# One table of the order of all steps, made anew with other step times for three kinds of steps: attention and two mixtures on one core

## The chip, the cores and the metric

The kernel runs on one core of one Trainium2 chip. What counts is the device time of one execution in microseconds (us), from the first to the last instruction with what the runtime puts around it; the figure of a kernel is the median over its runs.

## What is computed

The inputs are q, k and v for 4 batches of 8 heads, 576 positions and 64 columns, a vector s for each head, and the weights of two feed-forward layers over all 2304 tokens. The reference, cut to what matters (the causal mask, reshaping and small constants are left out):

```python
bias   = cum[..., None, :] - cum[..., :, None]          # cum: running sum of max(s, 0)
scores = q @ k.T / 8 + minimum(bias, 0)                  # causal
attn   = softmax(scores) @ v                             # then x = heads side by side, 2304 x 512

h = x @ w_in                                             # 512 -> 2048
x = (h - tanh(h)) @ w_out                                # 2048 -> 512

h = x @ w2_in                                            # 512 -> 1024
e = exp(h - max(h)); solu = h * e / sum(e)
out = layernorm(solu) * g_ln @ w2_out                    # 1024 -> 512
```

## The kernel before

**Number form.** A float32 operand is split into a high part (a cast to the matmul's own 32-bit form) and a low part (what the cast leaves), and each product is three matmuls: high by high, high by low, low by high. So almost every value that TensorE makes is read out of PSUM by ScalarE (ACT) or VectorE (DVE), cast ("hi"), and subtracted ("lo") before TensorE (PE) may use it again. `copy` (L293 and its neighbours) and `diff` (L317 on VectorE, L318 on GpSimd) are the helpers for that, so that those lines collect work of all stages.

**Attention.** Twenty jobs A0 to A19 (pairs of heads; the first eight jobs are two halves of one pair) of units with scores (L719), the bias and maximum (L736), the exponential (L747), row work on GpSimd (POOL, L751), transposes (L785) and the product with v in `weigh` (L825, after which `xs` at L835 and a store to DRAM give the next layer's input). During it the weights of the next layer are loaded in float32 ("cd") and split (`convert_w`, L403 to L421; the first instruction of a split is an ACT absolute value at L421, `ct<-cd`).

**First layer** (`expert1`). Nine blocks of 256 tokens. A step *h* of one chunk of 128 hidden columns is 12 matmuls of 256 columns (L872, into `t`); then come tanh on ACT (L877), the gate h - tanh h on VectorE (L881), the cast to `gh` on ACT (L293), the low part on VectorE or GpSimd (L317, L318), and two chunks later a step *x* of 12 matmuls (L895) into an accumulator. Chunks 0 to 7 run in two visits (Xa) into `acc`, some of them while attention still runs; their sums are kept in DRAM. Chunks 8 to 15 run last (Xb) into `big`, and `join` (L957, `xp`) adds the kept sums. The weights of chunks 8 to 15 (tiles `wb`) have no room until attention's buffers are given up: `att_close` does that after the last attention step, and their loads are issued behind it.

**Second layer.** For each block, `products` P0 to P8 forms the hidden values with seven products instead of eight (p1, p6, p5, p2, p3, p7, p4 in program order), each 6 matmuls of 512 columns (L1013). p1 and p2 add into one half of the PSUM tile `big`, p5 and p3 into the other; p6, p7 and p4 use a tile `b`. Between them stand small steps: copies of p1 and p5 to `hc` on ACT (k1, k5), the sum u2 (L1029), k15 (`hc<-hc`, L317), and u4 at L1044, which adds u2 into the half of `big` that p5 wrote and that p3 will add to. The weights of this layer are split by the same engines shortly before P0. `expert2`, E0 to E17 (128 tokens each), does the softmax form, the layernorm statistics and the reciprocal root: an integer first guess (L1100 to L1102) and three rounds of three tiny instructions on 128x1 tiles, `newton` (L1107 to L1109), on GpSimd or on VectorE. Its result is used by `fin` alone (ACT, L1134), after the four product steps *o* (L1129) of that tile; before those the tile is transposed (step *T*, L1115), cast and split (`cu`, `cd`, L1122).

**What sets the order.** Nothing is decided on the chip. `schedule` creates 3302 steps with their dependencies, and `Plan.order` reads the string `ORDER`: each base-36 word is three times the number of a step plus the number of the way it is done (which engine); `+n` is n filler matmuls on a tile `junk` (L562), which compute nothing that is used. The steps are emitted in that order, and each engine works off its instructions in the order in which they were emitted. The costs that stand in the calls of `add` and `any` are inputs of a planner that is not part of this file: here they are read by nothing that emits instructions.

Of the kernel before, what the change touches and what calls it, by code (L numbers as in the profile page):

```python
# [43 lines left out]
TB = 256  # L44
# [17 lines left out]
35o vi su wf vg vl wd vo wi sx v6 wl vr 11x 12o 13r 123 wo 12u wx 126 12r 129 399 vu 121 12y 130 13u 12c x0 vx 133 wr
140 159 x3 144 136 wu 13x 139 16f 146 13i 15c t6 149 15i 11r 12f 15f 15m 13c 14c 16i 13l 14o 13f 1rx 15o 16o x6 14f
15r 12i 16r 13o 14r 183 15u 34o x9 166 14i xf 14u ul xj 15x 16u 1eo 34r xl 34u 14l 1s0 34x xc 160 xo uo 350 169 163
18c 14x ur 353 xr xu 16c 18f uu 196 356 150 1f0 16l xx y3 153 16x 3df 35r 170 35u 39c 17c y0 y6 156 18i 3di 199 3dx
173 19f 18o 3dl 36l 19l 18m 18r 39f 3do 18u 39i 17l y9 17f 18x 1ex 3e0 1f3 176 3e3 3ds 19c 190 19o 17i yc 19r 39l 179
1a3 1ac 1f9 1l9 39o 17o 1bu 3e6 193 19u 1fc 1af 39r 1ll 1ff 1al 3ea 379 17r 1ai 1bx 3er 1fi 1ar 1ap 39u 3h0 1c0 1au
1f7 1ax 19j yf 1c3 1b9 36o 19x yi 3ef 1b0 1c9 yl 36r 1cc 17u 1c7 1cf 17x 1li 1a0 1ci 1a6 1b3 1a9 36u 1bc 1fl 1cr 1b6
1fr 1bf 36x 1bi 1fo 180 1fu 1lo 1gx 1fx 1ls 370 1if 1lu 1g0 37x 373 1lx 1h0 1cl 376 37c 1cu 1h3 1io 3ei 1cx 1ii 1g6
1g4 37f 1co 1g9 1m0 1d0 37i 1iu 1m3 1h6 1ha 3el 1is 37l 1m6 1yi 3eu 1d9 1m9 3eo 37o 1bl 1hc 1bo 37r 1d3 3f9 3ex 37u  # L70
1d6 3f0 3fo 1gc 3f3 1hf 1dc 1gf 1hi 3fc 3f6 1il 1br 1hu 3ff 3g6 1ix 3fi 1go 1j0 3b9 3fl 3fr 1jc 1df 3fu 1ru 3g3 1di
1hl 3fx 1dl 3g0 3g9 1dx 3gc 1yl 3gl 3gf 1do 3gi 380 1j3 1e0 383 1e6 1dr 1e3 386 1gi 3h3 1du 389 1gl 1e9 38c 1mc 3h6
38l 1ni 3h9 38f 1mf 1ec 3hc 1ml 3hf 1mi 1nr 1mr 1nv 1mu 1nx 38i 1nl 3bc 1mp 1gr 1s3 1mx 3bf 1ef 1hx 1n9 1ei 1ho 1gu
# [1239 lines left out]
```

## Time and profile before

| what | value |
| --- | --- |
| median of 3 runs | 791.61 us (791.07 to 792.75) |
| the profiled execution | 792.16 us |
| its span, first to last instruction | 790.4 us |
| PE busy | 771.3 us (98%) |
| DVE, ACT, POOL busy | 541.4, 412.6, 156.0 us |
| mean granted clock of TensorE | 0.999 of full speed |

The profile shows one execution. An engine counts as busy while an instruction of its runs; a matmul's end is modelled, so that a busy PE can still run its matmuls further apart or closer together. 1.76 us of the profiled execution lie outside the span. The waits are inferred from semaphores: a row "PE x <- DVE y" is time in which PE stood still until that instruction of VectorE was done.

### The profile page before, as it was taken

How to read it: one execution, taken by the hardware profiler on the slowest of the kernel's cores; microseconds unless marked ns; L12 is line 12 of the kernel's file. 1: busy time of each engine (PE TensorE's matmuls, PEld its weight loads, DVE VectorE, ACT ScalarE, POOL GpSimd, SP SyncE). 2: the span in 40 equal slices, each digit the busy share in tenths (PEclk: the TensorE clock that was granted, in tenths of full speed). 3: DMA queues.
4: the chain of work that ended last, by engine and by line, in shares of the span. 5: the costliest groups of instructions: out<-in, count | busy, mean ns of one | idle time of the engine just before them, and what ended most of it. 6: DMA issues, size and time to landing. Idle time of an engine off the chain costs nothing.

```text
span 790.4 us, 16621 instructions
## 1 busy us (share of the span) xinstructions
PE 771.3 (98%) x6235; PEld 681.0 (86%) x6235; DVE 541.4 (68%) x1521; ACT 412.6 (52%) x1028; POOL 156.0 (20%) x321
## 2 busy tenths in 40 slices
PE   8899999999999999999999999999999999999998
PEld 5565788888898899999999898888899899989876
DVE  6887988854554366985699998765465664564773
ACT  6779988766666445554355664333142333333332
POOL 4334433322331100000000001122041202021112
PEclk9999999999999999999999999999999999999999
DMA  6999979867445379875445431012012101201001
GB/s 189 300 284 252 329 219 290 271 184 215 123 121 165 105 226 292 278 244 181 160 131 183 136 111 48 15 54 92 16 43 65 41 15 66 95 1 41 15 27 41
DMA packets 90033, 111.90 MB, mean 142 GB/s; under 512 B 11792, under 2 KB 74256, under 8 KB 89952
## 3 DMA queue, kind: packets, MB, share of 16 engines
q1 hardware_dynamic: 89952, 110.83, 45.7%
q8 instruction: 49, 0.80, 0.4%
q14 instruction: 32, 0.26, 0.1%
HBM read 87.11 MB, written 23.70 MB: 140 GB/s over the span
## 4 chain that ended last, share of the span: by engine, by line
PE 80%; DVE 10%; ACT 4%; DMA 2%; issue 2%; SPq 1%; POOL 0%; ACTq 0%; DVEq 0%; POOLq 0%
PE t L872 20%; PE t L1129 12%; PE acc L895 11%; PE big L895 10%; PE big L1013 6%; PE t L825 5%; PE t L785 4%; PE b L1013 4%; PE t L719 4%; PE t L1115 2%; ACT U L747 1%; DVE ct L414 1%; DVE U L736 1%; DVE ct L409 1%; ACT pt L293 1%
## 5 line engine op out<-in xcount | busy, mean ns | idle before, releaser
L872 PE MATMUL t<-xb,wih 128*128 128x256 f32 x1152 | 203.4, 279 | 0.1
L872 PEld LDWEIGHTS t<-xb,wih 128*128 128x128 f32 x1152 | 175.6, 188 | 2.2 <-DVE m L736 0.3
L872 PE MATMUL t<-xb,wil 128*128 128x256 f32 x576 | 160.0, 278 | 0.0
L751 POOL TENSOR_SCALAR U<-U,r 128x256 f32<-128x256 f32 (+8 forms) x144 | 85.8, 608 | 174.5 <-DVE r L663 72.9
L872 PEld LDWEIGHTS t<-xb,wil 128*128 128x128 f32 x576 | 108.7, 189 | 0.0
L895 PE MATMUL acc<-gh,woh 128*128 128x256 f32 x576 | 104.7, 283 | 1.2 <-DVE gh L317 1.1
L895 PE MATMUL big<-gh,woh 128*128 128x256 f32 x576 | 101.2, 278 | 0.6 <-DVE xp L957 0.6
L881 DVE TENSOR_TENSOR g<-t,th 128x256 f32<-128x256 f32 x144 | 59.8, 418 | 52.4 <-ACT th L877 51.2
L293 ACT CAST gh<-g 128x256 fp32r<-128x256 f32 x144 | 58.0, 406 | 67.9 <-DVE g L881 30.1
L877 ACT ACTIVATE th<-t 128x256 f32<-128x256 f32 x144 | 55.0, 383 | 71.1 <-PE t L872 66.5
L895 PEld LDWEIGHTS acc<-gh,woh 128*128 128x128 f32 x576 | 87.7, 188 | 3.0 <-DVE gh L317 1.8
L747 ACT ACTIVATE U<-U,m 128x256 f32<-128x256 f32 (+8 forms) x144 | 80.3, 559 | 18.4 <-DVE m L736 17.8
L895 PEld LDWEIGHTS big<-gh,woh 128*128 128x128 f32 x576 | 87.9, 188 | 1.8 <-ACT th L877 0.7
L317 DVE TENSOR_TENSOR gh<-g,gh 128x256 fp32r<-128x256 f32 x130 | 56.4, 436 | 36.2 <-ACT gh L293 35.0
L895 PE MATMUL acc<-gh,wol 128*128 128x256 f32 x288 | 80.4, 279 | 0.2 <-DVE wol L317 0.2
L895 PE MATMUL big<-gh,wol 128*128 128x256 f32 x288 | 79.9, 278 | 0.0
L293 ACT COPY pt<-t 128x512 f32<-128x512 f32 (+4 forms) x160 | 61.2, 427 | 14.1 <-PE t L785 13.1
L736 DVE CUSTOM_DVE_ANT_0 U<-bc,t 128x256 f32<-128x256 f32 (+8 forms) x144 | 60.2, 441 | 5.7 <-PE t L727 3.0
L719 PE MATMUL t<-kn,q 64*64 64x288 f32 (+8 forms) x640 | 59.3, 422 | 1.8 <-ACT pt L293 0.9
L895 PEld LDWEIGHTS acc<-gh,wol 128*128 128x128 f32 x288 | 54.5, 189 | 0.4 <-DVE wol L317 0.4
L895 PEld LDWEIGHTS big<-gh,wol 128*128 128x128 f32 x288 | 54.2, 188 | 0.0
L1107 POOL TENSOR_SCALAR u<-y,va 128x1 f32<-128x1 f32 x45 | 20.9, 465 | 165.1 <-DVE y L1102 137.9
(115 smaller groups left out, 1432.5 us busy)
## 6 DMA issues: line engine op xcount, KB each, us to landing
xb<-xd SPq DMA_DIRECT2D x17, 1024.0 KB, 7.2
cd<-in_moe_w_in_dram SPq DMA_DIRECT2D x24, 512.0 KB, 5.5
cd<-in_moe_w_out_dram SPq DMA_DIRECT2D x24, 512.0 KB, 4.8
bc<-cum_d SPq DMA_DIRECT2D x32, 288.0 KB, 6.4
pd<-xp SPq DMA_DIRECT2D x18, 512.0 KB, 3.0
xp<-pd SPq DMA_DIRECT2D x18, 512.0 KB, 4.1
xd<-xs SPq DMA_DIRECT2D x16, 320.0 KB, 5.1
kn<-in_k_dram SPq DMA_DIRECT2D x16, 288.0 KB, 5.2
```

Of the source, the lines that this page charges most:

```text
L293: nc.scalar.copy(o, i)
L317: return self.any([("dve", t_dve(n, pair=True), lambda: nc.vector.tensor_tensor(*views(), op), "diff-dve"), ("pool", t_pool(n) + split, la ...
L719: nc.tensor.matmul(X[a][c, :z - a], lhsT=V["q"][r, o:o + 64], rhs=V["k"][r, a:z], start=True, stop=True, skip_group_check=True)
L736: nc.vector.tensor_tensor_reduce(out=X["u"][:, a:z], in0=V["bc"][:, n, a:z], in1=X[b][:, a - b:z - b], scale=-0.125, scalar=X["m"] if "m" ...
L747: nc.scalar.activation(out=X["u"][:, :nk], in_=X["u"][:, :nk], func=AF.Exp, scale=-1.0, bias=X["m"], accum_out=Y["s"][:, n:n + 1])
L751: eng.tensor_scalar(X["u"][:, :nk], X["u"][:, :nk], Y["r"][:, n:n + 1], 1.0, ALU.mult, ALU.mult)
L872: nc.tensor.matmul(ps, lhsT=w[l][:, k, f * 128:f * 128 + 128], rhs=xb[:, r, k, :], start=k == 0 and x == 0, stop=k == 3 and x == 2)
L877: nc.scalar.activation(out=X["th", f], in_=X["h", f], func=AF.Tanh)
L881: nc.vector.tensor_tensor(X["g", f], X["h", f], X["th", f], ALU.subtract)
L895: nc.tensor.matmul(X["acc"][:, m, :], lhsT=w[l][:, f, m * 128:m * 128 + 128], rhs=X["gh", f][:, r, :], start=f == c0 and m % 2 == 0 and x ...
L1013: nc.tensor.matmul(o, lhsT=self.x2[j][:, l, x, k], rhs=r[:, b, k, :], start=start and k == 0 and n == 0, stop=k == 1 and n == 2, skip_grou ...
L1129: nc.tensor.matmul(X["po"], lhsT=X["lt", k // 4][:, l, k % 4, :], rhs=r[:, k, :], start=k == 0 and a == 0, stop=k == 7 and a == 2)
```

## The change

The string `ORDER` is another one. Beside it the costs of three kinds of steps are changed: the h and x steps of `expert1` from 1405 to 1370 ns, the products and the output steps of the second layer from 1360 to 1366 ns, and `newton` on GpSimd from 1900 to 3200 ns. As nothing that emits instructions reads the costs, the program differs by the table alone. Of the table the diff is cut to its first line; lines behind the table stand one further down.

```diff
-0 f x 3 i 10 l u 49 7x p 4i r +22 13 4l 1u 16 2i 86 1a 1c 1x 39 bu 2l 20 2p 6 1f 23 2r 1i 3c 89 1l 2u 4d 26 2x bx 4f
...
+0 f 3 u i l x 49 4i 7x p r +20 13 10 1u 2i 16 86 1a 1c 1x 39 bu 2l 4d 6 2p 1f 20 3c 4l 2r 23 1i 4f 1l 89 3f 2u 26 2x
...
-                s = add("pe", t_pe(1405.0, 12 * TB), lambda f=f: h_part(f), ld + [w["ready"][2 * f]] + list(deps), acq=("ps",),
+                s = add("pe", t_pe(1370.0, 12 * TB), lambda f=f: h_part(f), ld + [w["ready"][2 * f]] + list(deps), acq=("ps",),
...
-                s = add("pe", t_pe(1405.0, 12 * TB), lambda f=f2: x2_part(f), [glo[f2], w["ready"][2 * f2 + 1]],
+                s = add("pe", t_pe(1370.0, 12 * TB), lambda f=f2: x2_part(f), [glo[f2], w["ready"][2 * f2 + 1]],
...
-            s = add("pe", t_pe(1360.0, 3072), go, deps + list(self.w2_all), acq=acq, rel=rel)
+            s = add("pe", t_pe(1366.0, 3072), go, deps + list(self.w2_all), acq=acq, rel=rel)
...
-        y = self.any([("pool", 1900, lambda: newton(nc.gpsimd), "rstd-pool"), ("dve", 2170, lambda: newton(nc.vector), "rstd-dve")],
+        y = self.any([("pool", 3200, lambda: newton(nc.gpsimd), "rstd-pool"), ("dve", 2170, lambda: newton(nc.vector), "rstd-dve")],
...
-            s = add("pe", t_pe(1360.0, 3072), lambda k=k: prod(k), [los[k // 4], self.w2_ready[8 + k], self.w2_ready[9 + k]],
+            s = add("pe", t_pe(1366.0, 3072), lambda k=k: prod(k), [los[k // 4], self.w2_ready[8 + k], self.w2_ready[9 + k]],
```

What the new table moves, counted over all steps: TensorE has the same 739 steps and 53 fillers instead of 49 (at the start 20 instead of 22). `newton` is on VectorE in all 18 tiles, where it was on GpSimd in 15 and on VectorE in 3. Of the `diff` steps 35 instead of 26 are on GpSimd. Two copies go from GpSimd to ACT.

**The last block of the second layer, PE.** `big` is the tile that p1, p2, p5 and p3 write, four rows each; `t<-idn,ct` are transposes of two tiles' halves. Before, from the end of p5 on:

```order
L1013 MATMUL big<-w2ih,x_10333 128x512 x2
L1013 MATMUL big<-w2il,x_10333 128x512
L1115 MATMUL t<-idn,ct 128x128 x8
L1013 MATMUL big<-w2ih,x_10333 128x512 x2
L1013 MATMUL big<-w2il,x_10333 128x512
L1013 MATMUL big<-w2ih,x_10333 128x512 x2
L1013 MATMUL big<-w2il,x_10333 128x512
L1013 MATMUL big<-w2ih,x_10333 128x512 x2
```

The last row is the start of p3, and the four rows ahead of it are p2. In the changed kernel, from p2 on:

```order
L1014 MATMUL big<-w2ih,x_10351 128x512 x2
L1014 MATMUL big<-w2il,x_10351 128x512
L1014 MATMUL big<-w2ih,x_10351 128x512 x2
L1014 MATMUL big<-w2il,x_10351 128x512
L1116 MATMUL t<-idn,ct 128x128 x8
L1014 MATMUL big<-w2ih,x_10351 128x512 x2
```

The transposes that stood ahead of p2 now stand between p2 and p3. In P0 to P8 there stood between p2 and p3: h, nothing, nothing, x, nothing, four h, h, two o, nothing. Now: h; two T, h and o; two T, three x and three h; thirteen steps; nothing; six h; two x; nothing; two T. In P4, P7 and P8 of the changed kernel (and in P4 before) u4 is emitted ahead of p2.

**The end of attention, ACT.** `xp<-acc` is the copy of a block's sums, and `ct<-cd` the first instruction that needs a weight loaded after `att_close`. Before:

```order
L293 COPY xp<-acc 128x1024
L877 ACTIVATE th<-t 128x256
L293 CAST gh<-g 128x256
L877 ACTIVATE th<-t 128x256
L421 ACTIVATE ct<-cd 128x512
L877 ACTIVATE th<-t 128x256
L293 CAST gh<-g 128x256 x2
```

In the changed kernel:

```order
L294 COPY xp<-acc 128x1024
L878 ACTIVATE th<-t 128x256
L294 CAST gh<-g 128x256
L878 ACTIVATE th<-t 128x256
L294 CAST gh<-g 128x256
L878 ACTIVATE th<-t 128x256
L422 ACTIVATE ct<-cd 128x512
L878 ACTIVATE th<-t 128x256 x2
```

One cast and one tanh of the first layer now stand ahead of the first instruction that needs the new weight.

**The last tile, VectorE.** Ahead of the low parts `cd` and `cu` of tile E17, before:

```order
L1092 BN_AGGR mv<-bn 128x2
L1100 TENSOR_SCALAR va<-mv 128x1
L1101 TENSOR_SCALAR y<-va 128x1
L1102 TENSOR_SCALAR y<-y 128x1
L1095 TENSOR_SCALAR ct<-ct,mv 128x1024
L1122 TENSOR_TENSOR cd<-t,cd 128x512
```

In the changed kernel:

```order
L1093 BN_AGGR mv<-bn 128x2
L1096 TENSOR_SCALAR ct<-ct,mv 128x1024
L1101 TENSOR_SCALAR va<-mv 128x1
L1102 TENSOR_SCALAR y<-va 128x1
L1103 TENSOR_SCALAR y<-y 128x1
L1108 TENSOR_SCALAR u<-y,va 128x1
L1109 TENSOR_SCALAR u<-u 128x1
L1110 TENSOR_TENSOR y<-y,u 128x1
```

After its last row two more rounds of the same three instructions follow, and then `cd` and `cu`. These nine stood on GpSimd.

## Rows read from the trace of the kernel before

**Rows 1.** The page: busy time of the engines; the chain's shares.

```profile
PE 771.3 (98%) x6235; PEld 681.0 (86%) x6235; DVE 541.4 (68%) x1521; ACT 412.6 (52%) x1028; POOL 156.0 (20%) x321
PE 80%; DVE 10%; ACT 4%; DMA 2%; issue 2%; SPq 1%; POOL 0%; ACTq 0%; DVEq 0%; POOLq 0%
```

**Rows 2.** Busy time by stretch; columns: length, five engines, granted clock, DMA share, GB/s.

```profile
0.00:40.00 40.00, 34.59 (x322) 22.58 (x323) 28.69 (x134) 28.22 (x91) 15.74 (x38) 1.00 0.85 247
40.00:80.00 40.00, 37.63 (x371) 25.39 (x371) 32.79 (x126) 33.29 (x94) 16.36 (x25) 1.00 1.00 266
...
280.00:300.00 20.00, 18.79 (x159) 18.13 (x158) 15.45 (x34) 9.61 (x23) 0.74 (x1) 1.00 0.75 238
300.00:340.00 40.00, 40.00 (x348) 40.00 (x347) 31.22 (x66) 20.42 (x45) 0.75 (x1) 1.00 0.86 281
...
400.00:440.00 40.00, 40.00 (x335) 39.23 (x334) 38.35 (x86) 22.98 (x51) 1.64 (x2) 1.00 0.40 123
...
520.00:560.00 40.00, 39.40 (x246) 35.02 (x247) 23.67 (x48) 11.91 (x23) 8.85 (x21) 1.00 0.18 60
```

**Rows 3.** PE's waits over the span: total us, times, longest us.

```profile
PE big L1013 <- DVE big L1044: 5.0, 6, 1.4
...
PE acc L895 <- DVE gh L317: 1.1, 2, 0.6
```

**Rows 4.** Timeline in P8, VectorE and PE: start, duration, instruction, idle before.

```profile
760.16 0.39 PE L1013 MATMUL big<-w2il,x 128*128 128x512 f32 x1
760.59 0.70 DVE L1044 TENSOR_TENSOR big<-big,u 128x512 f32<-128x512 f32 x1 [1.02 <-PE big L1013]
761.34 0.73 PE L1013 MATMUL big<-w2ih,x 128*128 128x512 f32 x2 [0.79 <-DVE big L1044]
```

**Rows 5.** Timeline in P0, the steps between p2 and p3.

```profile
442.67 0.58 ACT L293 COPY hc<-big 128x512 f32<-128x512 f32 x1
443.41 0.68 DVE L317 TENSOR_TENSOR hc<-hc 128x512 f32<-128x512 f32 x1
444.75 0.73 PE L1013 MATMUL big<-w2ih,x 128*128 128x512 f32 x2 [1.37 <-DVE big L1044]
```

**Rows 6.** Timeline of ACT at the end of attention.

```profile
279.94 0.39 ACT L877 ACTIVATE th<-t 128x256 f32<-128x256 f32 x1
283.87 0.67 ACT L421 ACTIVATE ct<-cd 128x512 f32<-128x512 f32 x1 [3.55 <-DMA cd<-in_moe_w_in_dram]
```

**Rows 7.** Timeline of PE in the same place.

```profile
286.05 0.39 PE L895 MATMUL acc<-gh,woh 128*128 128x256 f32 x1 [0.51 <-DVE gh L317]
...
288.26 0.39 PE L895 MATMUL acc<-gh,woh 128*128 128x256 f32 x1 [0.55 <-DVE gh L317]
```

**Rows 8.** The chain that ended last, in order of time: start, duration, what.

```profile
277.93 5.70 DMA cd<-in_moe_w_in_dram
...
297.01 5.44 PE acc L895 x48
...
331.47 5.65 PE acc L895 x48
...
402.14 7.19 PE t L872 x60
```

**Rows 9.** The first instruction of newton by engine: ns min/median/max, first and last start.

```profile
L1107 POOL TENSOR_SCALAR u<-y,va x45: 338/343/1383, 483.1 to 777.9; 128x1 f32<-128x1 f32 x45
L1107 DVE TENSOR_SCALAR u<-y,va x9: 265/273/275, 484.2 to 755.3; 128x1 f32<-128x1 f32 x9
```

**Rows 10.** Timeline: first and last instruction of one newton on GpSimd, one on VectorE.

```profile
483.10 0.50 POOL L1107 TENSOR_SCALAR u<-y,va 128x1 f32<-128x1 f32 x1 [30.62 <-DVE y L1102]
...
485.99 0.19 POOL L1109 TENSOR_TENSOR y<-y,u 128x1 f32<-128x1 f32 x1
...
753.93 0.27 DVE L1107 TENSOR_SCALAR u<-y,va 128x1 f32<-128x1 f32 x1
...
755.80 0.16 DVE L1109 TENSOR_TENSOR y<-y,u 128x1 f32<-128x1 f32 x1
```

More of the change, by code (lines that the diff above doesn't have):

```diff
@@ new lines @@
+37o 1fx 3el 1hi 1ml 37x 1hu 1mf 1ii 37r 3f9 1hl 1g9 1mr 1gc 1mp 37u 1il 1gf 1ho 1ix 1mi 3fo 1g4 1go 1j0 1mu 3ex 3eo
+1mx 1hr 3f0 1j3 3fc 3ff 3f3 1n0 1d0 3f6 3fr 1n9 3fu 3fi 1jc 3fx 1gi 1yi 1d3 3g6 1gl 3g1 1yl 1d9 1d6 3fl 1dc 3g3 3g9
+1ru 3gc 1df 1di 3gl 3bc 1dl 3bf 3gf 1dx 3h3 3gi 1do 380 3bi 1e0 3h6 383 1dr 3bl 1e3 1e6 1nc 3h9 1gr 1e9 1n3 1du 3bo
+3go 1gu 386 39x 3br 389 3hc 1jl 1n6 3bu 1nf 38c 1ni 253 1jo 3hg 38f 1s6 3gr 38l 1nr 1jr 256 1nl 38j 1ju 1nx 1jx 1ec
+1no 1nv 1s9 1yf 3gu 1o0 1sd 1o3 1of 3a0 1o6 3gx 1k0 3a3 1i3 1s3 3a6 1ef 1k3 3a9 1sf 1hx 1i6 3ic 1k6 1i0 3ac 1ki 1ei
@@ new lines @@
+25f 219 25j 106 21l 2ic 109 1sx 21c 263 1t0 21o 10c 1rl 266 21f 25l 1ro 3ix 21r 25o 1rr 10f 25r 21i 1t6 10r 269 26c
+1tc 1ta 3j0 10i 26i 26l 1t3 26g 259 25u 26o 1tf 1ti 26r 3jf 3j6 1tu 1tl 270 1to 110 3ji 1tx 10u 3jl 113 1tr 3ju 1u0
+3jo 3jr 10x 3j9 3ko 3jx 2bl 3k0 3k3 226 3k6 23c 22f 22j 22l 229 2bx 2ox 21u 23f 22c 2ou 10l 23l 23i 22o 25x 23o 3k9
+260 22r 2i6 23r 22u 23u 10o 233 3kr 23x 3kc 240 3kf 21x 220 3ki 249 236 223 3ku 22x 3kl 239 26u 24c 3kx 3nx 26x 2c0
+243 3l0 2c4 24i 3l3 24f 116 24l 246 230 2c6 2c9 2cc 2cf 1u3 2bu 119 1vl 11c 1u6 11f 279 1uc 1u9 2ii 1vo 24o 1ui 2il
@@ new lines @@
+1ug 1vu 1vr 1vy 1ul 1w0 27i 27m 1uo 2ip 27o 1w3 1ur 27c 273 2if 1w6 24r 3lo 1v0 24u 276 1w9 27f 24x 27r 2ir 1wi 27u
+1v3 2iu 2ix 3lr 1uu 27x 1wc 3lu 1v6 2j0 1wl 1ux 286 1wf 280 1v9 1wo 283 1wr 1vc 1vf 1vi 2j9 1wu 28f 2vi 1x0 1wx 2vf
+2ci 2ji 289 1x3 2j3 2jo 3l6 2jm 2jc 2or 1x6 1x9 2j6 2jf 1xc 3l9 2jr 1xf 3lx 2ju 2cl 28i 3m0 28c 2k6 1xi 28l 28o 3lc
+1xo 1xl 2jx 1xr 3lf 2k9 1xx 2k0 3m3 3li 1xu 1y0 2kc 2k3 3mx 3m6 3m9 3mc 3mi 3mf 3n0 3ml 3no 3mo 3mr 3o0 3mu 3q9 3n3
+3n6 3n9 3of 3nc 3o3 3o6 3ou 3oi 3ol 2co 3ox 2du 2cr 2p3 2cx 2cu 1y3 2d1 2p6 2dx 2d3 2pa 2pc 2e3 2e0 2pf 2e7 2pi 2d6
@@ new lines @@
+2e9 2d9 2pl 2ec 2dc 2fc 2ef 2p0 1y6 2dl 1y9 2er 2pu 2fl 3nf 2ei 1yc 2fp 2fr 2ff 2q3 2fi 2q7 2px 2eu 2do 2fu 2q0 2df
+2fx 3pc 3o9 2g0 2di 2ex 3oc 2dr 2g9 2q9 3p0 2g3 3si 3pf 2qc 2el 2qf 3ni 2g6 2qi 2eo 2qr 2gc 3oo 2f0 3or 2gf 3pi 2r0
+2f3 2f6 2gi 2r3 2f9 2r9 2r6 28r 2rd 2gl 2rf 2po 2gr 2go 3nl 290 2pr 294 28u 296 2gu 3qc 28x 3nr 2vc 2gx 3qr 299 2ri
+3p3 29c 2rl 3nu 2h0 3qf 3p6 29o 2h3 3qi 3p9 3qu 2h6 29f 3pr 3pl 2rx 3po 2hf 3qx 2h9 3ql 2ro 29i 2hc 3qo 2hi 2rr 29l
+2ho 3q0 2qu 2hl 2ql 3pu 2hr 2ru 2qo 2qx 3px 3r0 3r3 2vo 2wf 2vr 2xl 2vv 2vx 2wi 2si 3q3 2wl 2s6 2xu 3q6 2xy 2y0 2w0
@@ L160 @@
+7ar 7hc 72i 7hi 71i 72l 72o 7hl 6tf 7hu 7ho 71l 7hr 71o 7hx 7if 7i0 7i3 7i6 72r 730 7i9 7ic 7bl 733 6ti 7bo 7br 7ii
+6tl 72u 72x 7io 7au 7bu 7il 7ax 7ir 7bx 736 7iu 7b0 7c0 7ix 7j1 739 7c6 7c3 7j3 7ca 73c 73f 7cc 7cl 7cf 7j6 7ci 7co
+7cr 7cu 7jl 7j9 7jo 7jr 7cx 7jc 7ju 7jf 7jx 7d0 7k0 7ji 7d3 7k3 7lf 7k9 7k6 7b3 7kd 7d6 7d9 7kf 7ko 7ki 7li 7b6 7ll
+7kr 7b9 7ku 7lo 7bc 7kl 7lr 7lu 7kx 7lx 7bf 7m0 7bi 7mf 7m4 7m6 7l0 7m9 7mi 7l3 7mc 7ml 7l6 7mo 7l9 7lc 7mr 7mu 7mx
+7n0 7n3
 """
```

194 lines of the change are left out of this document (85 added, 109 removed).

## The prediction

> **What bounds the kernel now.** I read the page first. PE is busy for 771.3 of 790.4 us, and four fifths of the chain run on it [rows 1]: the matmuls' own time is the bound, and a table that keeps the same 739 steps can win back only what is not matmul. That is 19.1 us of idle time, plus the fillers, plus whatever the matmuls lose by running further apart than they must. The stretches [rows 2] say where it lies: 5.4 and 2.4 us idle in the first two of 40 us, 1.2 us between 280 and 300, some 0.6 us in a stretch such as 520 to 560, and nothing around 300 to 440. The waits [rows 3] name the largest single cause: p3 of the products waits for u4 (L1044), 5.0 us in six places.
>
> **Part 1: p3 waits for u4.** P8 shows the mechanism [rows 4]. The last matmul of p2 starts at 760.16 and runs 0.39; u4 starts at 760.59, right behind it, though VectorE had been idle for 1.02; p3 starts when u4 is done. u4 works on the half of `big` that p2 doesn't touch, so by the data it need not wait for p2. It does where it is emitted behind p2: the wait is on the tile. The price with nothing between p2 and p3 is the 0.79 of [rows 4], that is u4's 0.70 and two hand-overs. In P0 the copy k5 is emitted behind p2 too, and k5, k15 and u4 run in a row, 0.58, 0.68 and 0.70; one h stands between, and 1.37 are left [rows 5]. The new table puts work there, or u4 ahead of p2, in eight of nine products. The tightest are P6, with two x steps (an x step of 12 matmuls takes 5.44/4 = 1.36 [rows 8], so 2.72) against a chain of about 2.0, and P1, with two T, an h and an o against about 1.4. P0 has the same single h as before and keeps its 1.37. Gain: 5.0 - 1.4 = **3.6 us**, bounds 2.2 (two of the new covers fail) and 5.0 (P0's chain is shorter as well, since DVE has fewer weight parts to do beside it). This reading needs no estimate of any duration that the trace doesn't show, so I trust it most.
>
> **Part 2: the end of attention.** The load that `att_close` lets go lands at 277.93 + 5.70 = 283.63 [rows 8]. ACT's first instruction on it stands early in ACT's order, and ACT sits idle 3.55 us for it [rows 6], with tanh and casts queued behind. PE pays later: 0.51 and 0.55 for `gh` [rows 7], and a third, shorter delay inside the x step at 291; with the weight loads that start late at the same places I count 1.9 between 285 and 292, against the 1.2 that the stretch 280 to 300 shows as idle PE [rows 2]. In the new order one cast and one tanh stand ahead of that instruction, so that the low parts that PE needs next no longer hang on the load. Followed step by step with the durations of these rows, PE would come to the first x step that still hangs on a converted weight at about the time at which its low part is done, with no slack. Gain: **1.8 us**, bounds 0 (it waits there for as long as before) and 2.2.
>
> **Part 3: two rhythms of the matmuls.** Twelve matmuls of the same kind take different times in two places: 48 take 5.44 us at 297.01, that is 113.3 ns each, and 5.65 at 331.47, that is 117.7 ns; 60 take 7.19 at 402.14, partly at either [rows 8]. The granted clock is 1.00 in both [rows 2], so it is not the clock, and no wait is shown. The slow rhythm lasts from 320 to 406, begins at a step whose weights were loaded a little late, and ends at a step that waited. 86 us x (117.7 - 113.3)/117.7 = 3.2 us are lost there. Nothing in the table aims at it, and a trace of before can't say at which step the changed kernel falls into it or out of it. If it never does, 3.2 are won; if the slow rhythm lasts from 293 to 437, where the products begin, 144 us x 3.7% are lost instead of 86 x 3.7%, 2.1 more than before. I take **1.0 us** won, between the two ends and a little to the good side, since neither state has a cause in the table.
>
> **Part 4: the first 84 us.** Idle PE makes 7.8 us here, 5.4 and 2.4. The new order starts two fillers earlier and has 53 instead of 49; the units of the first jobs stand in another order, and the first h step comes 13 steps later on PE, so that less of the first layer is at hand to fill gaps, while later it catches up. ACT and DVE are at 28 and 33 of 40 us [rows 2], so gaps of PE come from chains of single units, which I can't time to a microsecond. I take a loss of **1.0 us**, bounds 2 won and 4 lost: the 5.4 idle in the first 40 us are the nearest row, and no reordering takes more than a part of it.
>
> **Part 5: newton on VectorE.** A newton takes 483.10 to 486.18 on GpSimd and 753.93 to 755.96, 2.03 us, on VectorE [rows 10]. Fifteen are moved, 15 x 2.03 = 30 us, into a stretch in which VectorE is busy for 23.67 of 40 us [rows 2]; from 480 on it would be at about 27.5 of 40. `fin` needs the result only after four o steps, 4 x 1.36 = 5.4 us, so newton itself is late nowhere. What pays is the work behind it on VectorE: gates and low parts, each kept from starting for up to 2.03. Where the table leaves less than that between a low part and its matmul, PE waits. Working through the chains from every PE step to the next that hangs on it, with the durations of this trace, I find about five steps in the second layer with less than 0.3 us to spare (p6 of P1, T of E4, E5 and E9, the first products of P8), as against three before. The trace of before shows waits of 0.5 to 0.8 where such a cover fails [rows 4, 7]. Two of five failing by 0.65 give a loss of **1.3 us**, bounds 0 and 3.5. Everything else is covered: the shifted copies and the nine `diff` steps on GpSimd hide behind two chunks of matmuls, and the tail (last matmul, `fin`, store) is as before.
>
> The trace shows GpSimd's first instruction of newton between 338 and 1383 ns, median 343 [rows 9]: now and then it is held up, by something that these rows don't name. The Trainium skill (SBUF — State Buffer, section "Who interferes with whom") says that a VectorE instruction with two SBUF inputs contends with a GpSimd instruction that reads SBUF, and that the later of the two is blocked until the first has finished. By that rule VectorE would also get back time that newton on GpSimd costs it now, and part 5 would be nearer to 0, the sum 1.3 lower; the rows show GpSimd held up and not VectorE, so I leave the sum as it is.
>
> **The sum.** 790.4 - 3.6 - 1.8 - 1.0 + 1.0 + 1.3 = 786.3 us of span. The profiled execution took 1.76 more than its span, 792.16, and lies 0.55 above the median of the runs: 786.3 + 1.76 - 0.55 = **787.5 us**.
>
> **The rivals.**
> *Newton blocks the low parts.* One mechanism: VectorE works in order, so a 2.03 us block that lands between a cast and its low part delays an x, T or o step by what exceeds its cover. It decides from a cover below the low part's chain plus 2.03. If 10 of the 15 expose 1.2 us, that is 12 us lost against the 5.4 won in parts 1 and 2: 795 us. For it: 18 of 18 now sit on VectorE, which is also where u4, u2 and k15 run. Against it: that stretch leaves VectorE 16 of 40 us idle [rows 2], and only five steps have covers that thin. 12 in 100. The Trainium skill (TensorE: Matmul & The Clock Gate, section "Architectural detail: the array is 16× 32×32, not 1× 128×128") calls VectorE's queue strictly first in, first out; the rows here agree, since u4's late start in [rows 4] shows VectorE waiting at an instruction and taking nothing from behind it.
> *The gains are spent in front.* The first 84 us lose 4 and the slow rhythm runs on to 437, or one of both with part 2 failing: span 790.4 - 3.6 - 1.8 + 4.0 + 2.1 = 791.1, hence 792.3, and between 790 and 793 for the milder forms. For it: both terms are the ones that I can only bound. Against it: both must go the wrong way. 20 in 100, of which about 6 end above 793.2.
> *The table makes no difference.* The matmuls are the bound, and each wait that is taken away reappears at the next thin place, 791.6. Against it: u4's wait is removed by six covers that have a microsecond or more to spare. 6 in 100.
> My forecast has the remaining 62; of these a few end just inside the bound of no change.
>
> **Chances and range.** About 0.2%, 1.6 us, is what a measurement of this kernel can tell from no change: 790.0 to 793.2. Faster: nearly all of the forecast and a little of the second rival, 0.63; within: 0.18; slower: the first rival and the worst of the second, 0.19. The range: all terms at their good ends together would give some 781 (parts 1 to 4 at 4.4, 2.2, 3.2 and 0, part 5 at 0: 790.4 - 9.8 + 1.2 = 781.8, and I allow 0.3 more); up to the second rival with a thin part of the first, 794.0.
>
> **What would show it.** Part 1: the row "PE big <- DVE big" falls from 5.0 in six places to about 1.4 in one, P0's. Part 2: ACT's wait for `cd` is shorter, and PE has no wait of 0.5 for `gh` between 284 and 292. Part 3: pieces of the chain with 48 matmuls of 256 columns at 5.44 or 5.65, and for how long. Part 4: idle PE and fillers in the first two stretches of 40 us. Part 5: all newton rows on VectorE, VectorE near 27 of 40 us from 480 on, new PE waits for `gh`, `cd` or `cu`; if they make over 5 us, the first rival is right. I am wrong in kind if the time rises although p3's waits are gone and VectorE shows no new waits: then the cost lies in attention or in the rhythm.

## The result and the profile after

The changed kernel takes 782.84 us (median of 6 runs, 778.76 to 785.02) against 791.43 us of the kernel before (6 runs, 787.65 to 792.75): ratio 0.989, 95% interval 0.9857 to 0.9923. It is 8.6 us faster, where 4.1 were forecast; the time lies inside the range of 781.5 to 794.0, near its lower end. The profiled execution took 780.84 us with a span of 779.1, so it is one of the quicker ones, as that of before, 792.16, was one of the slower: the two profiles lie 11.3 us apart, and 2.7 of these are not the change's but belong to the two executions. Where they come from is the business of the first experiment.

The page of the changed kernel, the lines of [rows 1]:

```profile
PE 766.1 (98%) x6239; PEld 676.9 (87%) x6239; DVE 563.9 (72%) x1647; ACT 410.2 (53%) x1030; POOL 119.7 (15%) x193
PE 88%; DVE 4%; DMA 3%; ACT 2%; SPq 1%; issue 1%; POOL 0%; DVEq 0%; POOLq 0%; ACTq 0%
```

VectorE has 22.5 us more to do (newton, less what moved the other way), GpSimd 36.3 less, and PE carries 88% of the chain where it carried 80%.

Busy time by stretch, the columns of [rows 2]:

```profile
0.00:40.00 40.00, 35.27 (x318) 22.63 (x322) 28.79 (x130) 27.31 (x88) 13.16 (x36) 0.96 0.88 246
40.00:80.00 40.00, 38.20 (x394) 26.23 (x386) 33.37 (x136) 35.29 (x103) 18.87 (x30) 1.00 1.03 268
...
280.00:300.00 20.00, 20.00 (x175) 19.96 (x175) 14.45 (x29) 8.97 (x22) 1.29 (x1) 1.00 0.97 313
300.00:340.00 40.00, 40.00 (x356) 40.00 (x355) 34.29 (x75) 22.51 (x49) 0.74 (x1) 1.00 0.84 278
...
480.00:520.00 40.00, 40.00 (x240) 35.35 (x238) 31.52 (x85) 14.32 (x28) 1.48 (x2) 1.00 0.09 34
520.00:560.00 40.00, 39.18 (x219) 33.55 (x218) 24.96 (x62) 11.49 (x21) 2.84 (x3) 1.00 0.17 55
560.00:600.00 40.00, 40.00 (x251) 35.63 (x250) 30.57 (x80) 15.06 (x30) 5.94 (x6) 1.00 0.09 32
```

PE's idle time falls from 5.4 to 4.7 and from 2.4 to 1.8 us in the first two stretches, and from 1.2 to nothing between 280 and 300. Between 300 and 340 PE is full in both, and yet 356 matmuls run in it instead of 348: that is the rhythm. VectorE is busy for 25 to 31.5 of 40 us between 480 and 600. The granted clock of the first stretch is 0.96 where before has 1.00: between 25 and 30 us it is 0.71 in the mean, just after PE has stood still for 2.1 us for a load of `kn`. The second profile of the changed kernel, in experiment 1, has neither that wait nor that fall, so both belong to this execution.

PE's waits, as in [rows 3] (total us, times, longest):

```profile
PE t L720 <- DMA kn<-in_k_dram: 2.1, 1, 2.1
...
PE acc L563 <- POOL junk L558: 1.1, 1, 1.1
PE big L1014 <- ACT hc L294: 0.7, 1, 0.7
PE big L1014 <- DVE big L1045: 0.6, 1, 0.6
...
PE t L1130 <- DVE cd L1123: 0.4, 1, 0.4
```

The wait of p3 for u4 is down from 5.0 us in six places to 0.6 in one. New are 0.7 for a copy (`hc`) and 0.4 for a low part `cd`. The 1.1 for `gh` of [rows 3] is gone.

To compare stages across kernels I cut each profile at two points that all of them have: the end of attention's last matmul, and the first matmul of P0. The matmuls of 256 columns (h and x) that lie in a stretch are taken off at 113.3 ns each, and what they take above that (intervals under 140 ns alone, so that waits don't count) is shown by itself as "rhythm". In us:

| profile | attention, without h and x | its end to P0, waits and the like | same, rhythm | P0 to the last matmul |
| --- | --- | --- | --- | --- |
| before | 178.9 | 2.6 | 3.4 | 350.2 |
| changed | 176.8 | 0.5 | 0.4 | 345.8 |

The experiments below fill further lines of this table. The rest of the text takes its numbers from it: attention, the stretch behind it, and the part from P0 on are the three places of the gain.

### The profile page after: what moved, and what is told of

It reads as the page before. It is cut to its first block, busy times and chain, and to the rows that moved or that the text cites. A ratio compares the mean times of both kernels' runs of the same rounds, so it can differ in the third digit from the quotient of the medians.

```text
span 779.1 us, 16644 instructions
## 1 busy us (share of the span) xinstructions
PE 766.1 (98%) x6239; PEld 676.9 (87%) x6239; DVE 563.9 (72%) x1647; ACT 410.2 (53%) x1030; POOL 119.7 (15%) x193
## 4 chain that ended last, share of the span: by engine, by line
PE 88%; DVE 4%; DMA 3%; ACT 2%; SPq 1%; issue 1%; POOL 0%; DVEq 0%; POOLq 0%; ACTq 0%
PE t L873 24%; PE big L896 12%; PE acc L896 12%; PE t L1130 12%; PE big L1014 6%; PE t L826 6%; PE t L720 5%; PE t L786 4%; PE b L1014 4%; PE t L1116 2%; DMA bc<-cum_d 1%; DMA cd<-in_moe_w_out_dram 1%; ACT U L748 1%; DMA kn<-in_k_dram 1%; DVE U L737 0%
## 5 line engine op out<-in xcount | busy, mean ns | idle before, releaser
L752 POOL TENSOR_SCALAR U<-U,r 128x64 f32<-128x64 f32 (+8 forms) x144 | 82.9, 589 | 164.7 <-DVE r L664 54.2
L896 PE MATMUL acc<-gh,woh 128*128 128x256 f32 x576 | 102.3, 280 | 0.0
L294 ACT CAST gh<-g 128x256 fp32r<-128x256 f32 x144 | 58.3, 406 | 66.4 <-DVE g L882 31.5
L748 ACT ACTIVATE U<-U,m 128x64 f32<-128x64 f32 (+8 forms) x144 | 80.1, 558 | 21.3 <-DVE m L737 20.9
L318 DVE TENSOR_TENSOR gh<-g,gh 128x256 fp32r<-128x256 f32 x124 | 53.9, 439 | 27.2 <-ACT gh L294 26.1
L737 DVE CUSTOM_DVE_ANT_0 U<-bc,t 128x64 f32<-128x64 f32 (+8 forms) x144 | 60.2, 441 | 8.8 <-PE t L728 6.1
L319 POOL TENSOR_TENSOR gh<-g,gh 128x256 fp32r<-128x256 f32 x20 | 16.6, 830 | 314.6 <-ACT gh L294 248.8
```

What stands on the lines that cost most here:

```text
L294: nc.scalar.copy(o, i)
L318: return self.any([("dve", t_dve(n, pair=True), lambda: nc.vector.tensor_tensor(*views(), op), "diff-dve"), ("pool", t_pool(n) + split, la ...
L737: nc.vector.tensor_tensor_reduce(out=X["u"][:, a:z], in0=V["bc"][:, n, a:z], in1=X[b][:, a - b:z - b], scale=-0.125, scalar=X["m"] if "m" ...
L748: nc.scalar.activation(out=X["u"][:, :nk], in_=X["u"][:, :nk], func=AF.Exp, scale=-1.0, bias=X["m"], accum_out=Y["s"][:, n:n + 1])
L752: eng.tensor_scalar(X["u"][:, :nk], X["u"][:, :nk], Y["r"][:, n:n + 1], 1.0, ALU.mult, ALU.mult)
L896: nc.tensor.matmul(X["acc"][:, m, :], lhsT=w[l][:, f, m * 128:m * 128 + 128], rhs=X["gh", f][:, r, :], start=f == c0 and m % 2 == 0 and x ...
```

## The experiments

**1. Both kernels again, unaltered.** The question was whether the two rhythms of [rows 8] belong to the program or to the execution.

```diff
 (no edit: the kernel before, the changed kernel)
```

> The kernel before again, unaltered, for a second profile. Theory (which of the two rhythms the 256-column matmuls run in, 113.3 or 117.7 ns, is settled anew in each execution at the steps that follow a transpose or a wait): the long stretch without transposes, some 290 to 430 us, is in the other rhythm for another part of its length than the 86 us of the first profile, and the span moves with it by up to 5 us while the waits of PE stay the same rows within 0.5 us. Rival (the program fixes it): 117.7 ns from 320 to 406 again.

> The changed kernel again, unaltered, for a second profile and as the neighbour of the run with newton on GpSimd. Theory that the 117.7 ns rhythm of the matmuls starts and ends by chance: its profile shows 256-column matmuls at 117.7 ns over other stretches than the first profile did, and the runs spread over 5 us or more. Rival (the rhythm is set by the program): the same stretches at 113.3 as in the first profile, runs within 2 us. Time in both cases 0.986 to 0.993 of the kernel before.

The second profile of before answers nothing: that one execution took 2682 us, nearly every 256-column matmul in it 420 ns apart, and the other runs of the same kernel 789.7 to 794.4. The second profile of the changed kernel does answer, for that kernel. Its chain, in order of time, between 302 and 330:

```profile
302.18 2.83 PE t L873 x24
305.00 1.41 PE acc L896 x12
...
316.31 5.65 PE acc L896 x48
321.96 7.07 PE t L873 x60
```

The same steps in the first profile of the changed kernel:

```profile
302.62 2.72 PE t L873 x24
305.34 1.36 PE acc L896 x12
...
316.22 5.44 PE acc L896 x48
321.66 6.80 PE t L873 x60
```

One program, the same steps at the same time, and 117.7 ns a matmul in one execution, 113.3 in the other. From attention's end to P0 the rhythm costs 6.1 us in the second profile and 0.4 in the first; the spans are 783.3 and 779.1. Profiles whose order is that of the changed kernel up to P0 show 0.4, 6.1, 0.1, 5.2 and 5.2; those with the order of before 3.4, 2.4, 1.3, 3.3 and 0.2. The 0.1 and one of the 5.2 come from the same chip, one shortly after the other. So in this stretch the rhythm differs from execution to execution, and its mean is not lower with the new order. That is 3 of the 11.3 us between the first two profiles, and 5.7 us between the two profiles of the changed kernel; it can make most of the 778.8 to 785.0 of its runs, but the runs without a profile don't show it. The runs of the second measurement spread over 4.2 us, where I had expected 5. Outside that stretch the program has its part: behind P0 both profiles of the changed kernel fall into the slow rhythm at the same five steps (at 478, 514, 569, 604 and 652 us in the first, 4.2 to 4.3 later in the second), each behind transposes, and the rhythm, counted as in the table, costs 1.4 us there in both. What decides it in the long stretch is open: the traces show it change only where the even row of 256-column matmuls is broken, by other matmuls, by a wait or by one interval of some 140 to 230 ns, and now to the one side, now to the other.

**2. u4 emitted first.** The kernel before, with nothing moved on any engine: only in the order in which the two engines' steps are emitted, u4 (and what it needs) goes ahead of p2. In P1 (`5m9` is p2, `5m3` u4):

```diff
-5fi 5m6 5du 5m9 5m3 5e3 5e6
+5fi 5m6 5du 5m3 5m9 5e3 5e6
```

> The kernel before with the emission alone changed: in eight products u4 (and k5, k15 where they stood behind it) is emitted ahead of p2; the order of the instructions on every engine is the same as before, row by row, only the wait of u4 for p2's end goes. Theory (u4 waits for p2 because both write the tile big): the row 'PE big <- DVE big' falls from 5.0 us to under 0.7, and the time falls by 3.5 to 4.6 us, ratio about 0.995. Rival (the wait is for something else, or the 5 us come back at the next thin place): time within 1 us of the kernel before, the waits move to other rows.

It became slower: 807.94 us against 791.04, ratio 1.0193 (1.0165 to 1.0221). PE's largest waits:

```profile
PE big L1013 <- DVE big L1044: 14.1, 8, 3.0
PE acc L895 <- DVE gh L317: 2.0, 3, 0.9
```

and the timeline of P3 (start, duration, engine, instruction, idle before):

```profile
564.28 0.39 PE L1013 MATMUL big<-w2il,x 128*128 128x512 f32 x1
...
564.71 0.59 ACT L293 COPY hc<-big 128x512 f32<-128x512 f32 x1
...
565.33 0.69 DVE L317 TENSOR_TENSOR hc<-hc 128x512 f32<-128x512 f32 x1
565.93 0.69 DVE L1044 TENSOR_TENSOR big<-big,u 128x512 f32<-128x512 f32 x1
...
566.68 0.73 PE L1013 MATMUL big<-w2ih,x 128*128 128x512 f32 x2 [2.01 <-DVE big L1044]
```

The matmul at 566.68 is p2. It now waits for u4, though it writes the half of `big` that u4 doesn't touch, and with it for k5 and k15: 2.01 us, where p3 had waited 0.63. The tile is what the wait goes by, as the prediction said, but it binds whichever of the two is emitted second. My expectation held only half of that, and neither it nor its rival foresaw a loss. The profiled execution was the quickest of its six, 802.46; in it the row grew by 9.1, and P0 to the end takes 360.3 us instead of 350.2. The 5.5 us that the median lies above it are in no profile. The mean granted clock of the other five runs is 0.991 to 0.993, that of the profiled one 0.998; 0.006 of some 807 us is 4.8 us (an estimate from these figures), so a clock that was lower somewhere could account for most of it. Where it was lower, and whether the new order brings that about, stays open. So u4 ahead of p2 is no cure in itself: the changed kernel can do it in P4, P7 and P8 because other steps stand between p5 and p2 there.

**3. A cover for three products.** The kernel before, with p2 ahead of the transposes in P1, P2 and P8. In P2 (`5vu` is p2, `5pl` and `5pc` the two T):

```diff
-5vl 5vr 5pl 5vu 5pc 5w0 5w3 5pf 5vx
+5vl 5vr 5vu 5w0 5w3 5pl 5pc 5pf 5vx
```

> The kernel before with p2 ahead of the transposes in P1, P2 and P8, so that two or three T stand between p2 and p3; nothing else is moved. Theory (p2 and u4 wait for each other in the order of emission, because both write the tile big, and what helps is work between p2 and p3): the three waits of 0.79 at P1, P2 and P8 go, 'PE big <- DVE big' falls from 5.0 to about 2.6, and the time falls by 1.5 to 2.4 us, of which P1 may give back 0.6 because its o steps follow the transposes sooner. Rival (the wait comes back elsewhere): no difference.

793.46 us against 791.73, ratio 1.0013 (0.9993 to 1.0033): no gain. PE's waits say why.

```profile
PE big L1013 <- DVE big L1044: 2.7, 3, 1.4
PE big L1013 <- ACT hc L293: 2.0, 3, 0.7
```

The row of u4 fell by 2.3, as expected, and 2.0 stand in a new row: p2 now comes right behind p5, and k5, which reads `big`, is emitted ahead of it, so p2 waits 0.7 for that copy, three times. It is the same tile a third time. Work between p2 and p3 pays only if p2 doesn't wait for k5 in its turn. Either p2 is emitted ahead of k5 as well, and then about 2 us of other work is needed between p2 and p3 for k5, k15 and u4: that is what the new table has in P1 (TTho), P2, P3 and P6. Or other work stands between p5 and p2 and covers k5: so in P5, where six steps behind p2 then cover u4. In P8 of the changed kernel two o steps stand ahead of p2 and two T behind it:

```profile
742.37 0.59 ACT L294 COPY hc<-big 128x512 f32<-128x512 f32 x1 [1.08 <-PE big L1014]
...
742.99 0.70 DVE L1045 TENSOR_TENSOR big<-big,u 128x512 f32<-128x512 f32 x1
...
744.91 0.62 PE L1014 MATMUL big<-w2ih,x 128*128 128x512 f32 x2
...
746.28 1.03 PE L1116 MATMUL t<-idn,ct 128*128 128x128 f32 x8
...
747.07 0.71 PE L1014 MATMUL big<-w2ih,x 128*128 128x512 f32 x2
```

The o steps between p5 and p2 cover k5 and u4, done at 743.69; p2 at 744.91 and p3 at 747.07 wait for nothing.

**4. Newton on the other engine, in both kernels.** In the 15 tiles that differ, each newton at its place in the order; the word of E1's, in before and in the changed kernel:

```diff
-5ff
+5fg
```

```diff
-5fg
+5ff
```

> The kernel before with newton on VectorE in all 18 tiles, each at its old place in the order. Theory (newton is covered, VectorE has the room): within 1 us of the kernel before, up to 1.5 us slower. Rival A (the move itself makes the changed kernel faster, since newton on GpSimd takes longer and disturbs VectorE): 2 to 5 us faster. Rival B (the 2.03 us block holds up low parts): 4 us slower or more, with new waits of PE for gh, cd or cu.

> The changed kernel with newton back on GpSimd in the 15 tiles where it was before. Theory: within 1 us of the changed kernel (782 to 784). Rival A (the gain comes from this move): 785 to 788. Rival B (newton on VectorE costs the changed kernel something): 779 to 781.

Both became slower, and both theories were missed. The kernel before with newton on VectorE: 801.59 against 791.04, ratio 1.0122 (1.01 to 1.0143). The changed kernel with newton on GpSimd: 788.98, ratio 0.9959 (0.9943 to 0.9976) to before, where the unaltered one beside it had 784.55 and 0.99, 4.4 less. From P0 to the end the profiles take 359.0 instead of 350.2, and 348.8 instead of 345.7 (the second profile of the changed kernel). The waits of the first:

```profile
PE big L1013 <- DVE big L1044: 4.3, 6, 0.8
PE t L1129 <- DVE cd L1122: 2.9, 4, 1.2
PE t L1115 <- DVE ct L1095: 2.4, 2, 1.6
```

The o steps wait for low parts and the transposes for the centred values, which stand behind newton on VectorE: the first rival of the prediction, in the order that had no room for it. Such waits make some 6 of its 8.8 us; the rest no row names. The second has, on GpSimd, ACT and PE:

```profile
540.52 0.19 POOL L1110 TENSOR_TENSOR y<-y,u 128x1 f32<-128x1 f32 x1
540.87 0.74 POOL L319 TENSOR_TENSOR xp<-xp 128x256 f32<-128x256 f32 x1 [0.16 <-DMA out_dram<-o]
...
541.64 1.04 ACT L294 CAST x<-xp 128x1024 fp32r<-128x1024 f32 x1 [2.62 <-POOL xp L319]
...
542.74 0.49 PE L1014 MATMUL b<-w2ih,x 128*128 128x512 f32 x1 [0.87 <-ACT x L294]
544.00 0.50 PE L1014 MATMUL b<-w2ih,x 128*128 128x512 f32 x1 [0.76 <-DVE x L318]
...
546.34 0.73 PE L1014 MATMUL big<-w2ih,x 128*128 128x512 f32 x2 [0.92 <-ACT hc L294]
```

In the unaltered changed kernel beside it (second profile) the same difference on GpSimd starts at

```profile
536.17 0.74 POOL L319 TENSOR_TENSOR xp<-xp 128x256 f32<-128x256 f32 x1 [31.80 <-DVE va L1101]
```

that is 4.7 us sooner, while `xp`'s earlier parts are only 0.8 us apart. Newton stands ahead of a difference `xp` that the new table gives to GpSimd, ACT waits 2.62 for it, and the product's operands come late; at 581 a low part `gh` on GpSimd comes 0.90 late as well. So neither engine is the better one for newton by itself; the engine and the order belong together, and a change of the one without the other costs 4.4 us in the changed kernel and 10.6 in the one before by the medians, 3.1 and 8.8 by the profiles from P0 on.

**5. The conversions at the end of attention.** The kernel before, with the first conversions of chunks 12 and 15 behind the four tanh, casts and low parts among which they stood (`4px` is the first):

```diff
-3xo 3xr 4px 3yi 4q0 3y3 3y6 3xu 4q3 3y9 3xx 3zi 41o 3yl 4q6 4rx 3yo 4q9 3yf 3zl 4s0 4ju 4qc 3yc
+3xo 3xr 3yi 3y3 3y6 3xu 3y9 3xx 3zi 41o 3yl 3yo 3yf 3zl 4ju 3yc 4px 4q0 4q3 4q6 4rx 4q9 4s0 4qc
```

> The kernel before with the first conversions of weights that are loaded after attention (chunks 12 and 15) moved behind the four tanh, casts and low parts of the first layer that they stood between; nothing else is moved. Theory (ACT waits for that load with the first layer's work queued behind it): PE's waits for gh at 286 to 292 go, the time falls by 1.5 to 2.2 us. Rival (PE waits for the same low parts a little later, because the conversions then stand in front of the next ones): within 0.7 us of the kernel before.

792.74 us against 791.73, ratio 1.001 (0.9989 to 1.0032): the rival. The waits at 286 and 288 of [rows 7] are gone, and one of 1.51 stands a few steps later:

```profile
291.12 0.38 PE L895 MATMUL acc<-gh,woh 128*128 128x256 f32 x1 [1.51 <-DVE gh L317]
```

In the changed kernel ACT still sits idle for the first load behind `att_close`, which is one of `w_out` there, 2.63 us:

```profile
280.54 0.38 ACT L878 ACTIVATE th<-t 128x256 f32<-128x256 f32 x1
283.55 0.67 ACT L422 ACTIVATE ct<-cd 128x512 f32<-128x512 f32 x1 [2.63 <-DMA cd<-in_moe_w_out_dram]
```

and PE doesn't notice. Its chain there:

```profile
276.36 9.52 PE t L873 x84
285.88 4.08 PE acc L896 x36
```

Seven h steps in a row, 9.52 us, need nothing of ACT, and the three x steps behind them follow without a gap; before, five h stood there and then x steps that hung on the late low parts. The two hybrids of experiment 6 with a seam at the end of attention fit this: with seven h steps in a row PE has no wait in this place, with four it has 2.7 us of waits for `gh` between 284 and 291. So moving ACT's work alone doesn't help, and what does goes with the number of h steps that PE has ahead of the x steps. No run moved those alone, so that this is the cause is argued and not shown.

**6. Halves of the one table and of the other.** Four kernels take one order up to a point and the remaining steps in the order of the other: the point is the end of attention (behind `4hr`) or P0 (ahead of `5br`). The first words behind the points, from before to the order of the changed kernel:

```diff
-2oi 2ol 2oo 4hr 3wu 4pu 4ru 3x6 3wx
+2oi 2ol 2oo 4hr 3x6 3x9 3xc 3xf 3xi
...
-50x 5br 51o 5si 510 51r 5bu
+50x 5br 5si 5sl 510 5bu 5c0
```

> The order of the kernel before up to the first product, P0, and from there the order of the changed kernel; nearly the same steps are done at that point in both, so that the seam costs nothing. Theory (the largest part of the gain lies behind P0: six waits of p3 become one, and nothing is given back for newton): from P0 to the last matmul 345.7 us instead of 350.2, time 785.5 to 788. Rival A (the part in front of P0 makes the gain): 790 to 792. Rival B (it all lies behind P0): 782 to 785.

> The complement: the order of the changed kernel up to P0, then that of the kernel before. Theory (attention gains 1 to 3 us and the end of attention 2): 786.5 to 789.5, and from P0 on the waits of p3 of the kernel before, 5.0 us in six places. Rival A (the part in front of P0 makes the gain): 783 to 785. Rival B: 790 to 792.

> The order of the kernel before up to the end of attention, and from there the remaining steps in the order of the changed kernel. Theory (of the changed kernel's 8 us some 2 come from attention and 6 from what follows: the close 2, u4 4): 784 to 787.5. Rival A (most of the gain lies in attention): 788 to 791. Rival B (the later part needs the earlier one, since the two orders have a different number of first-layer steps done at the seam): above 791.

> The order of the changed kernel up to the end of attention only, then that of the kernel before. Theory (attention in the new order has two more steps of the first layer done at its end, at the same time): 788.5 to 790.5. Rival (attention gains nothing beyond its scatter of some 2 us): 791 to 793.

| order of steps | median us, before beside it | ratio (interval) | gain us |
| --- | --- | --- | --- |
| before to P0, then changed | 787.89, 792.54 | 0.9938 (0.9917 to 0.9958) | 4.7 |
| changed to P0, then before | 788.07, 792.54 | 0.994 (0.9918 to 0.9961) | 4.5 |
| before to attention's end, then changed | 784.37, 791.73 | 0.9907 (0.9878 to 0.9936) | 7.4 |
| changed to attention's end, then before | 789.62, 792.54 | 0.9978 (0.9958 to 0.9998) | 2.9 |

The two halves at P0 make 4.7 and 4.5, together 9.2, about the whole. All four medians lie in the range that the theory gave; of the 5.0 us of waits that the second was to keep, 4.3 stand, in the same six places. Their profiles, in the table of stages (us):

| profile | attention, without h and x | its end to P0, waits and the like | same, rhythm | P0 to the last matmul |
| --- | --- | --- | --- | --- |
| before to P0, then changed | 182.4 | 3.0 | 0.2 | 345.5 |
| changed to P0, then before | 176.3 | 0.6 | 5.2 | 350.0 |
| before to attention's end, then changed | 178.0 | 0.2 | 2.8 | 345.5 |
| changed to attention's end, then before | 176.3 | 5.4 | 2.7 | 349.5 |
| changed, second profile | 175.7 | 0.2 | 6.1 | 345.7 |

Behind P0 the two orders differ by 3.7 to 4.7 us in these profiles and the first two; the profile of experiment 5, which has the old order there, took 350.9, so that it is 5.4 at most. The stretch behind attention is worth 2.3 (the means of six profiles with the old order there, that of experiment 5 among them, and six with the new are 2.8 and 0.5; the 5.4 of the last hybrid is not among them: behind its seam only four h steps are left ahead of the x steps, and PE waits there as experiment 5 tells). Attention scatters: 178.0 to 182.4 in seven profiles with the old order, 175.7 to 177.5 in six with the new. The two groups don't overlap, but by the runs the gain there is only just clear of no change (0.9958 to 0.9998), and the last hybrid pays its seam out of it.

PE's waits of the first hybrid and of the second behind P0 say the same, in this order:

```profile
PE big L1013 <- DVE big L1044: 0.6, 1, 0.6
```

```profile
PE big L1013 <- DVE big L1044: 4.3, 6, 0.8
```

**7. Two more moves.** The changed kernel with an x step ahead of p3 in P0 (`5so`, `5ci` is p3), and the copy of p1 in P3 one cast earlier on ACT (`65i`):

```diff
-520 523 5ci 529 606 52c 5tu 52f 5cl 5cx 5so
+520 523 5so 5ci 529 606 52c 5tu 52f 5cl 5cx
...
-6d6 5xr 5yl 6da 6e3 65c 6do 6dr 65i 5yo
+6d6 5xr 5yl 65i 6da 6e3 65c 6do 6dr 5yo
```

> The changed kernel with two moves for the two waits of the products that are left: an x step ahead of p3 in P0, and the copy of p1 in P3 one cast earlier on ACT. Theory: PE's waits at 437 (0.64) and 539 (0.74) fall to 0 and 0.3, the time by 1.0 us against the changed kernel, which the comparison can hardly tell: 782 to 784.5. Rival (the waits move to the next step): same waits elsewhere, no gain.

782.41 us (6 runs, 779.37 to 784.54), ratio 0.9872 (0.9845 to 0.9899) to before. The wait for u4 is gone altogether and that for `hc` is 0.5:

```profile
PE big L1014 <- ACT hc L294: 0.5, 1, 0.5
PE t L873 <- DVE g L882: 0.5, 1, 0.5
```

The second row is new: further on, at 454 us, an h step now waits for a gate. So the rival has its share, a wait moved to a later step. From P0 to the end it takes 345.4 us instead of 345.7. That is the direction, but the medians 782.41 and 782.84 can't be told apart, and its profile had the quick rhythm (0.1). That it is quicker than the changed kernel isn't shown.

## Why the prediction was right, and where not

**What bounds the kernel** was read rightly: no matmul went away, PE is as full as before, and the gain lies in the three places that the stretches of [rows 2] pointed at. In the products and behind attention it is waits that went; of attention's 3 us idle time is only 1.2. The forecast has the direction and about half of the size, 4.1 of 8.6; the largest piece of what it missed is part 4.

**Part 1, u4: right.** Forecast 3.6 won; the row fell from 5.0 to 0.6, with 0.7 new for `hc` beside it, 3.7 net. P0 keeps its wait, though shorter, 0.6 and not the 1.37 of [rows 5]. The reason, a wait that goes by the tile, is shown by experiment 2, in which it turns round. One clause of the step was wrong: u4 ahead of p2 is no cure by itself (experiment 2), and work between p2 and p3 is one only where p2 doesn't wait for k5 instead (experiment 3).

**Part 2, the end of attention: right in size, wrong in cause.** Forecast 1.8, measured 2.3 by the means of the profiles. The step that failed is "so that the low parts that PE needs next no longer hang on the load": experiment 5 did just that and gained nothing, since the wait moved to the next low part. What the new order has is seven h steps ahead of the x steps instead of five. That 1.8 is near 2.3 is therefore luck.

**Part 3, the rhythm: right that nothing in the table aims at it, wrong in the amount by design.** I took 1.0 won between two ends. Experiment 1 shows no systematic gain at all: between attention and P0 it costs 0.2 to 3.4 us in five profiles with the old order and 0.1 to 6.1 in five with the new. Had I only compared the two first profiles, I should have credited the change with 3 us that belong to the execution.

**Part 4, the first 84 us: wrong in sign, and the largest miss.** Forecast 1.0 lost, measured 1 to 3 won (the mean of the profiles goes from 179.9 to 176.6, 0.4 of it rhythm; the hybrid with the new attention alone gains 2.9, the one without it falls 1.2 short of the whole). Idle PE in the first 160 us falls from 8.3 to 7.1. I had argued that fewer first-layer steps early leave less to fill gaps with. The reading behind it was off: by the two tables the first h step is TensorE's 48th step instead of its 43rd, five later and not 13, and the second is one earlier. And the order was shifted as a whole: at the end of attention, at the same time (274.2 and 274.8 us), two more of them are done. The step that failed is judging by the order of the first jobs instead of counting what is done at a later point that both share. Where within attention the rest comes from isn't settled; from one transpose to the next 1.3 us less are spent in the first profile, which no experiment took apart.

**Part 5, newton: 1.3 lost was too much; for the fifteen that moved the rows show nothing.** The step that failed is the five thin covers of which two were to fail. The one new row of that kind, 0.4 for `cd` at an o step at 479, stands behind a newton that is on VectorE in both kernels, and it is there too (0.37 at 484) with the other fifteen back on GpSimd. So no row is the price of the fifteen; the 0.6 for `xp` that before had is gone. The rival was a real mechanism: experiment 4 gives it 9 to 11 us, near the 12 of the rival's price, where the order has no room. Here it has room, in an order in which newton stands on VectorE throughout.

On VectorE and GpSimd holding each other up the prediction read its rows too narrowly: in the trace of before both are held up. Each pair below, both from the second layer, is the instruction that came first and the one that had to wait:

```profile
450.96 1.52 POOL L318 TENSOR_TENSOR w2ol<-ct,w2oh 128x512 fp32r<-128x512 f32 x1 [23.41 <-ACT w2oh L293]
451.25 1.52 DVE L317 TENSOR_TENSOR gh<-g,gh 128x256 fp32r<-128x256 f32 x1
...
549.97 1.22 DVE L317 TENSOR_TENSOR x<-xp,x 128x1024 fp32r<-128x1024 f32 x1
550.16 1.24 POOL L1107 TENSOR_SCALAR u<-y,va 128x1 f32<-128x1 f32 x1 [4.05 <-DVE y L1102]
```

A low part `gh` on VectorE takes 421 ns in the mean of the 104 that no GpSimd instruction overlaps; this one takes 1518 and ends 0.3 us after GpSimd's. The first instruction of newton takes 343 ns in the median; this one takes 1237 and ends 0.2 us after VectorE's. But newton's own 128x1 instructions cost these low parts nothing: the 11 low parts `gh` that overlap one take 421 ns too. So moving newton won nothing back there. GpSimd's wide instructions do hold up low parts: the 15 that overlap one take 553 ns in the mean.

**The sum.** Forecast span 786.3 = 790.4 - 3.6 - 1.8 - 1.0 + 1.0 + 1.3. With the measured terms, 790.4 - 4.5 (P0 to the end: 3.7 of part 1, 0.6 for `xp`, less 0.4 for `cd`, and 0.6 that no row names) - 2.3 - 3.0 = 780.6, give or take what the rhythm does; the six runs have spans of 777.0 to 783.2. Two sums of the prediction are off. The good end of the range takes 4.4 and 0 for parts 1 and 4, whose own bounds are 5.0 and 2 won: with these it is 779.2 and not 781.5, so the measured 782.84 lies less near the edge than it looks. And 12 us lost against 5.4 won are 798.2, not the 795 of the first rival. *The gains are spent in front* was the wrong rival to fear, and *The table makes no difference* fell with the measured time and with experiment 6.

## What to carry to other kernels

Where two instructions write different halves of one tile, the wait between them goes by the tile, and the one that is emitted second waits: emitting them the other way turns the wait round and can make it longer, so put work in between on both sides (splitting the tile would be the other way; no run here tried it). A step's engine and its place in the order are one decision; moving newton to the other engine at its old place cost 4 to 11 us here, in both directions. Before two profiles are compared, take off what differs between two executions of the same program, and measure a stage between points that both share; halves of the one order and of the other then show quickly in which stage a change pays.

## What the runs showed of the hardware

The same stretch of 256-column matmuls, at a granted clock of 1.00, ran at 113.3 ns in one execution and at 117.7 in another, for up to 160 us at a time; in the stretch from attention to P0 that is worth up to 6 us, 0.8% of the kernel, enough for most of the spread of its runs. I had not been able to say whether the rhythm follows from the program: in that stretch it doesn't, behind P0 both profiles of the changed kernel turn slow at the same five steps. VectorE's low parts and GpSimd's wide instructions hold each other up, 1518 instead of 421 ns in the longest case, while the 128x1 instructions of newton on GpSimd cost VectorE's low parts nothing. And one execution of the kernel before had nearly every such matmul 420 ns apart, with a granted clock that the profile gives as 1.0, and took 2682 us.
